# Another list of steps for the main phase of a one-core attention and feed-forward kernel

## The chip, the cores and the metric

The program runs on one core of a Trainium2 chip. The metric is the device time of one execution in microseconds (us), as the median of several executions. Engines are named as in the profile: PE (matmuls), PEld (its weight loads), DVE, ACT, POOL and SP (which issues nearly all DMAs).

## The reference, cut to what matters

A row vector x of width 512 goes through an attention with 32 heads of width 16 that all share one key and one value head, and through a gated feed-forward layer of inner width 1376. A sigmoid gate g, one number for each of the 2048 rows, mixes both.

```python
g = sigmoid((x * gate_w).sum(-1, keepdims=True))
q = (x @ wq).reshape(B, S, H, Dh).transpose(0, 2, 1, 3)      # S 2048, H 32, Dh 16
k, v = x @ wk, x @ wv                                        # one head for all
p = softmax(einsum("bhqd,bkd->bhqk", q, k) * Dh ** -0.5)
a = einsum("bhqk,bkd->bhqd", p, v).transpose(0, 2, 1, 3).reshape(B, S, H * Dh) @ wo
b = (gelu(x @ w_gate) * (x @ w_up)) @ w_down                 # inner width 1376
out = g * a + (1 - g) * b
```

## The kernel before, in words

The rows are cut into four groups of 512. A prologue of some 82 us computes the queries of all groups (written to HBM as `scr`), the keys `kp`, the values `v1` and `v2` and a first piece of the feed-forward layer. Then comes the main phase, which both halves of the reference share, and a short tail (the output projection of the last group).

Attention in the main phase goes by units: a unit `u` is one row group and four of the 32 heads, so there are 32 units, and each runs over 16 key chunks of 128. For a unit and a key chunk there are two **score steps** (letter S in the list). A score step is a pair of matmuls (L751), each on one half of PE's 128 rows, that write 128 x 1024 scores into two banks of PSUM, and one exponential on ACT (L754) that reads them and writes a tile `p`. There are three such bank pairs: numbers 0 and 1 take the scores in turn; number 2 takes them where the list has a Z in place of an S. There are 1024 score steps. Then comes one **value step** (letter V) for each unit and key chunk: four matmuls (L821) beside each other, each on 32 of PE's columns, that add the product of `p` and the values to the unit's accumulator `acc`. There are 512 of them; the profile shows each as 8 matmuls, the program's order as 4. After the last value step of a unit, `norm` copies the accumulator with DVE (L765, L775) and divides by the row sums in further pieces of DVE work, kept in the queue `bg`.

The feed-forward layer and the output projection make 77 **jobs**. A job multiplies two pairs of operands at once, into the banks `z` (bank pair 2) and `y`; numbers are split into a high and a low part, so that each product takes three passes. A **pass step** (letter F, L519) is a pair of matmuls, one for `z` and one for `y`, each on one half of PE's rows. A job goes over its passes twice: in the second half `z` and `y` change places between the two halves of the rows, for which the first matmul of the second half waits for a small memset on POOL (L527) that waits for the first half. There are three kinds of job: gate jobs (24 pass steps, followed by a gelu on DVE and ACT, L544 to L560), down jobs (18 or 12 pass steps, followed by two additions on DVE, L624) and output jobs (24, L634). Weights and rows are split into high and low parts while a job runs: DVE casts the high part (L201), POOL subtracts it (L202); `slot` puts one such piece of work behind every third pass step. At the end of a row group `reload_x` loads the next group's rows as tiles `xst` and splits them into `xh` and `xl` in the same way, during the last two down jobs of the group.

What stands in which order on PE is written out in the table `PLAN`, 78 lines, one for each job and one ahead. `play` reads a line word by word:

```python
            if t[0] in "SZ":
                for _ in range(k):
                    score(t[0] == "Z")
            elif t[0] == "V":
                visit(k)
            elif t[0] == "H":
                ...
                pairs = pair_mm(z, y, X, Y)
            elif t[0] == "F":
                for _ in range(k):
                    next(pairs)
            else:
                job[1](z, y)
```

H opens a job, R closes it (the else branch: DVE's work on `z` and `y` is issued), T issues the gelu's tanh on ACT, and a number behind a letter repeats it. All engines take their instructions in the order in which `play` issues them, so the table sets the order on DVE, ACT, POOL and SP too.

Of the kernel before, what the change touches and what calls it, by code (L numbers as in the profile page):

```python
# [20 lines left out]
S = 2048  # L21
D = 512
H = 32
DH = 16
F = 1376
# [17 lines left out]
PB = 12  # L43
PLAN = [
# [78 lines left out]
]  # L123


# [811 lines left out]
```

## Time and profile before

| | |
|---|---|
| median of 3 runs | 1246.28 us (1244.94 to 1249.26) |
| the profiled execution | 1246.9 us, its span 1244.8 us |
| PE busy | 1237.2 us (99%) |
| ACT busy | 1031.7 us (83%) |
| DVE busy | 526.2 us (42%) |
| POOL busy | 215.6 us (17%) |
| granted PE clock | 0.999 |

The first line holds times of whole executions. The others come from one execution that the profiler recorded. A PE that is busy all the time need not do its work at full pace: a matmul's end is modelled, so the pace is read from the starts of the steps.

### The profile page before, as it was taken

Reading aid. Unit: us, or ns where it says so; the run is one execution under the profiler, and the core shown is the slowest. Engines: PE = TensorE matmul, PEld = TensorE weight load, DVE = VectorE, ACT = ScalarE, POOL = GpSimd, SP = SyncE. Lnnn points to the kernel's source line nnn. Section 1 sums busy time; section 2 is a strip of 40 time slices with the busy share of each in tenths; the row PEclk is TensorE's granted clock in tenths of the full one; section 3 lists DMA queues with packets and bytes.
Section 4 is the critical chain, followed back from the end, with each engine's and each line's share of the span. In section 5 each row is a group of like instructions: output and inputs, shape, how many; then the busy total and the mean of one; then the engine's idle time right before and its main releaser. Section 6 shows DMA issues by size and latency. Waiting matters only on the chain.

```text
span 1244.8 us, 23618 instructions
## 1 busy us (share of the span) xinstructions
PE 1237.2 (99%) x9742; PEld 657.5 (53%) x9742; DVE 526.2 (42%) x844; ACT 1031.7 (83%) x1127; POOL 215.6 (17%) x265
## 2 busy tenths in 40 slices
PE   9999999999999999999999999999999999999998
PEld 6775555454544554545454555554544555455544
DVE  7872553525423144443443234162455126253334
ACT  5448888988888888888888788888889888898894
POOL 5420311212210120211230021120231011121100
PEclk9999999999999999999999999999999999999999
DMA  8541201103201211101210221010211201010000
GB/s 329 193 149 43 83 14 65 40 23 107 73 15 31 70 40 40 65 24 40 89 53 14 74 65 40 14 65 16 92 58 40 74 14 65 14 58 34 14 1 34
DMA packets 28317, 73.89 MB, mean 59 GB/s; under 512 B 4208, under 2 KB 4464, under 8 KB 28208
## 3 DMA queue, kind: packets, MB, share of 16 engines
q1 hardware_dynamic: 27664, 71.32, 17.1%
q8 instruction: 77, 1.26, 0.4%
q0 software_dynamic: 256, 0.79, 0.2%
q10 hardware_dynamic: 288, 0.26, 0.1%
q14 instruction: 32, 0.26, 0.1%
HBM read 57.41 MB, written 14.94 MB: 58 GB/s over the span
## 4 chain that ended last, share of the span: by engine, by line
PE 92%; issue 1%; POOL 0%; DVE 0%; ACT 0%; DMA 0%; SPq 0%; POOLq 0%
PE acc L821 38%; PE s L751 23%; PE y L519 17%; PE z L519 13%; PE wos L504 1%; POOL xl L202 0%; DVE acc L634 0%; DMA Q<-scr 0%; PE wof L504 0%; ACT p L754 0%; SPq L364 0%; ACT sq L551 0%; SPq L363 0%; POOLq L202 0%; POOL mark L527 0%
## 5 line engine op out<-in xcount | busy, mean ns | idle before, releaser
L754 ACT ACTIVATE p<-s 128x1024 f32<-128x1024 f32 x1024 | 977.4, 1026 | 150.3 <-PE s L751 139.7
L821 PE MATMUL acc<-p,v 128*32 128x512 f32 x4096 | 496.4, 599 | 0.0
L751 PE MATMUL s<-Q,kp 51*128 51x512 f32 x2048 | 397.2, 421 | 1.0 <-DMA Q<-scr 0.9
L751 PEld LDWEIGHTS s<-Q,kp 51*128 51x128 f32 x2048 | 183.7, 184 | 258.0 <-ACT p L754 167.3
L821 PEld LDWEIGHTS acc<-p,v 128*32 128x32 f32 x4096 | 106.7, 109 | 239.2 <-issue 231.2
L527 POOL MEMSET mark<- 1x1 f32 x77 | 7.6, 99 | 890.0 <-PE y L519 874.0
L519 PE MATMUL z<-xh,gh 64*128 64x512 f32 x312 | 122.9, 394 | 0.0
L519 PE MATMUL y<-xh,gh 64*128 64x512 f32 x312 | 122.8, 394 | 0.0
L519 PE MATMUL z<-xl,gh 64*128 64x512 f32 x312 | 122.2, 392 | 0.3 <-POOL xl L202 0.2
L519 PE MATMUL y<-xl,gh 64*128 64x512 f32 x312 | 122.4, 392 | 0.0
L544 DVE COPY gs<-z 128x512 f32<-128x512 f32 x39 | 27.0, 692 | 225.4 <-PE z L519 214.9
L519 PE MATMUL z<-xh,gl 64*128 64x512 f32 x312 | 121.9, 391 | 0.0
L519 PE MATMUL y<-xh,gl 64*128 64x512 f32 x312 | 121.9, 391 | 0.0
L202 POOL TENSOR_TENSOR gl<-st,gh 128x512 fp32r<-128x512 f32 x80 | 107.4, 1361 | 36.5 <-DVE gh L201 35.7
L624 DVE SCALAR_TENSOR_TENSOR acc<-z,gc,acc 128x512 f32<-128x512 f32 x24 | 18.0, 751 | 130.9 <-PE z L519 128.3
L519 PE MATMUL z<-dh,hh 64*128 64x512 f32 x176 | 69.2, 393 | 0.0
L519 PE MATMUL y<-dh,hh 64*128 64x512 f32 x176 | 69.1, 393 | 0.0
L519 PE MATMUL y<-dl,hh 64*128 64x512 f32 x176 | 68.9, 392 | 0.0
L519 PE MATMUL z<-dl,hh 64*128 64x512 f32 x176 | 68.9, 391 | 0.0
L519 PE MATMUL z<-dh,hl 64*128 64x512 f32 x176 | 68.8, 391 | 0.0
L519 PE MATMUL y<-dh,hl 64*128 64x512 f32 x176 | 68.7, 391 | 0.0
L519 PEld LDWEIGHTS y<-xh,gl 64*128 64x128 f32 x312 | 57.7, 185 | 8.4
(174 smaller groups left out, 1536.9 us busy)
## 6 DMA issues: line engine op xcount, KB each, us to landing
st<-wf SPq DMA_DIRECT2D x40, 768.0 KB
scr<-q SPq DMA_DIRECT2D x16, 512.0 KB
Q<-scr SPq DMA_DIRECT2D x64, 128.0 KB
Q<-scr SPq DMA_DIRECT2D x64, 64.0 KB
out<-acc SPq DMA_DIRECT2D x16, 256.0 KB
xr<-xT SPq DMA_DIRECT2D x6, 512.0 KB
xst<-xT SPq DMA_DIRECT2D x12, 256.0 KB
st<-wf SPq DMA_DIRECT2D x5, 256.0 KB
```

The lines of the kernel that those rows point to most:

```text
L202: eng_l.tensor_sub(lo, src, hi)
L504: nc.tensor.matmul(ps, a, b, start=(first and q == 0), stop=(last and q == len(terms) - 1), skip_group_check=True)
L519: mm = nc.tensor.matmul(ps, a[rs], b[rs], start=(half == 0 and q == 0), stop=(half == 1 and q == len(X) - 1), skip_group_check=True)
L527: relay = nc.gpsimd.memset(mark, 0.0).ins
L544: nc.vector.tensor_copy(gs, g)
L624: nc.vector.scalar_tensor_tensor(o, ps, w, o, op0=ALU.mult, op1=ALU.add)
L751: nc.tensor.matmul(ps[:, j * TG : (j + 1) * TG], kp[rs, kc * P : (kc + 1) * P], Q[u][rs, pr], start=True, stop=True)
L754: nc.scalar.activation(p, ps, AF.Exp, bias=0.0, scale=SCALE)
L821: nc.tensor.matmul(accp[u][32 * j : 32 * j + 32], vt[:, kc], pb[s, j // 2][:, (j % 2) * TG : (j % 2 + 1) * TG], start=(kc == 0), stop=(kc ...
```

## The change

All 78 lines of `PLAN` are replaced, nothing else. The new lines hold the same numbers of score steps (1024), value steps (512), pass steps (1608) and jobs (77) in the same order of jobs; the steps are interleaved in another way. Two lines out of the 78, the one of the last down job of the second row group and the last one:

```diff
-    "f: H F4 S F2 S V S F6 R S2 V3 S",
+    "f: H F3 S F3 S V S F3 S F3 R S V Z S2 V3 Z S2 V2 S",
...
-    "f: H F3 S F3 S V S F2 S F4 R S V Z S2 V2 S V3",
+    "f: H F5 S F S V S F3 S F3 R S V5",
```

Counted over both tables (S and Z both as score steps; a block is a row of equal steps that follow each other on PE):

| | before | now |
|---|---|---|
| value blocks of 1, 2, 3, 4, 5 steps | 106, 117, 36, 16, 0 | 103, 91, 58, 12, 1 |
| value blocks in all | 275 | 265 |
| score blocks of 1, 2, 3 steps | 634, 54, 94 | 658, 15, 112 |
| pass blocks of 3 steps, of all | 268 of 508 | 362 of 521 |
| places where a score and a pass step meet | 1015 | 1041 |
| score steps in bank pair 2 (Z) | 119 | 112 |

PE at the end of the main phase, from the last pass step on, before. `s` are the banks of the scores, `acc` is the accumulator of the last unit, `wos` the first of the tail's four results:

```order
L519 MATMUL z<-dh_12869,hl_13223 128x512
L519 MATMUL y<-dh_12869,hl_13223 128x512
L751 MATMUL s<-Q_12767,kp 128x512 x2
L821 MATMUL acc_13186<-p,v_76 32x512 x4
L751 MATMUL s<-Q_12767,kp 128x512 x6
L821 MATMUL acc_13186<-p,v_76 32x512 x8
L751 MATMUL s<-Q_12767,kp 128x512 x2
L821 MATMUL acc_13186<-p,v_76 32x512 x12
L504 MATMUL wos_13452<-woh,oh_11623 128x512
```

The same place now:

```order
L519 MATMUL z<-dh_12965,hl_13247 128x512
L519 MATMUL y<-dh_12965,hl_13247 128x512
L751 MATMUL s<-Q_12720,kp 128x512 x2
L821 MATMUL acc_13162<-p,v_76 32x512 x20
L504 MATMUL wos_13452<-woh,oh_11542 128x512
```

Three value blocks of one, two and three steps have become one of five; the sixth value step and four score steps stand further ahead.

DVE at the reload of the third row group's rows, before. `xst2_0` to `xst2_3` are the four loaded pieces of the rows, `xh2` their high parts, `acc14` is the accumulator of unit 14, and the lines L624 are the additions behind the last two down jobs of the second group:

```order
L201 CAST xh2_6864<-xst2_1_6736 128x512
L624 SCALAR_TENSOR_TENSOR acc1_4152<-z_6915,gc_79,acc1_4152 128x512
L624 SCALAR_TENSOR_TENSOR acc1_4152<-y_6916,gc_79,acc1_4152 128x512
L795 CAST oh13_6991<-nt12_6229 128x512
L799 TENSOR_TENSOR ol13_6992<-nt12_6229,oh13_6991 128x512
L765 COPY n014_6995<-acc14_6670 128x512
L201 CAST xh2_6864<-xst2_2_6868 128x512
L201 CAST xh2_6864<-xst2_3_6959 128x512
L766 TENSOR_SCALAR nt14_6996<-n014_6995,mk_80 128x512
```

The same place now:

```order
L795 CAST oh13_7005<-nt12_6220 128x512
L799 TENSOR_TENSOR ol13_7006<-nt12_6220,oh13_7005 128x512
L765 COPY n014_7009<-acc14_6639 128x512
L201 CAST xh2_6911<-xst2_1_6811 128x512
L624 SCALAR_TENSOR_TENSOR acc1_4265<-z_6974,gc_79,acc1_4265 128x512
L624 SCALAR_TENSOR_TENSOR acc1_4265<-y_6975,gc_79,acc1_4265 128x512
L201 CAST xh2_6911<-xst2_2_6915 128x512
L201 CAST xh2_6911<-xst2_3_7026 128x512
L766 TENSOR_SCALAR nt14_7010<-n014_7009,mk_80 128x512
```

The copy of the unit's accumulator stood between the additions of the last down job and the casts of the last two pieces; now it stands ahead of those additions.

144 rows, old and new, of the table PLAN are left out of this document.

## The prediction

> **What bounds the kernel now.** I read the page first, then PE's waits, then the timeline of PE and ACT in a piece of the main phase, last the one place where PE's waits name another engine. The page gives the span, each engine's time and the chain that ended last:
>
> ```profile
> span 1244.8 us, 23618 instructions
> ...
> PE 1237.2 (99%) x9742; PEld 657.5 (53%) x9742; DVE 526.2 (42%) x844; ACT 1031.7 (83%) x1127; POOL 215.6 (17%) x265
> ...
> PE 92%; issue 1%; POOL 0%; DVE 0%; ACT 0%; DMA 0%; SPq 0%; POOLq 0%
> ...
> L754 ACT ACTIVATE p<-s 128x1024 f32<-128x1024 f32 x1024 | 977.4, 1026 | 150.3 <-PE s L751 139.7
> L821 PE MATMUL acc<-p,v 128*32 128x512 f32 x4096 | 496.4, 599 | 0.0
> ```
>
> PE is never idle and makes 92% of the chain. ACT is second: its 1024 exponentials fill 977.4 us, and it stood idle 150.3 us ahead of them, nearly all of it (139.7) until PE had written scores. So ACT waits for PE. PE's own list of waits is short. Its two rows with lines of the main phase (engine and line, what it waited for, total, count, longest):
>
> ```profile
> PE s L751 <- DMA Q<-scr: 0.9, 1, 0.9
> ...
> PE z L519 <- POOL xl L202: 0.2, 1, 0.2
> ```
>
> The first happened once, ahead of the first score steps, and both tables begin alike; no DMA was waited for after that, so SP's changed order costs nothing as long as loads are issued as far ahead as now. The second comes back below. So the main phase is as long as PE's steps at PE's pace, and what a new order of the same steps can change is what PE pays for going from one kind of step to another, and the waits. The timeline of PE shows both prices (start, duration, what, count):
>
> ```profile
> 407.81 0.40 PE L751 MATMUL s<-Q,kp 51*128 51x512 f32 x2
> 408.05 0.39 PE L519 MATMUL z<-woh,oh 64*128 64x512 f32 x1
> ...
> 408.74 0.40 PE L751 MATMUL s<-Q,kp 51*128 51x512 f32 x2
> ...
> 410.61 0.40 PE L751 MATMUL s<-Q,kp 51*128 51x512 f32 x2
> 410.94 2.78 PE L821 MATMUL acc<-p,v 128*32 128x512 f32 x24
> 413.65 0.51 PE L751 MATMUL s<-Q,kp 51*128 51x512 f32 x2
> 413.99 0.39 PE L519 MATMUL y<-woh,oh 64*128 64x512 f32 x1
> ...
> 417.47 0.41 PE L751 MATMUL s<-Q,kp 51*128 51x512 f32 x2
> 417.81 1.07 PE L821 MATMUL acc<-p,v 128*32 128x512 f32 x8
> 418.81 0.97 PE L751 MATMUL s<-Q,kp 51*128 51x512 f32 x6
> 419.71 2.78 PE L821 MATMUL acc<-p,v 128*32 128x512 f32 x24
> 422.42 0.50 PE L751 MATMUL s<-Q,kp 51*128 51x512 f32 x2
> 422.76 0.39 PE L519 MATMUL z<-xh,gh 64*128 64x512 f32 x1
> ```
>
> From the score step at 407.81 to the next at 408.74 lie that step and three pass steps (the first is shown), 0.93 us, 0.2325 each: a score step costs what a pass step costs, and going between the two costs nothing. A value block is different. The chain of waits has blocks of three and of four value steps:
>
> ```profile
> 108.62 2.71 PE acc L821 x24
> 132.75 3.57 PE acc L821 x32
> ```
>
> One more value step is 0.86 us. From 410.61 to 413.99 are two score steps and a block of three: 3.38 - 2 x 0.2325 - 3 x 0.86 = 0.335 us over. From 417.47 to 422.76 are five score steps and blocks of one and three: 5.29 - 5 x 0.2325 - 4 x 0.86 = 0.69, so 0.34 each. If I take the price of a value step from the same rows, (2.71 - 1.00) / 2 = 0.855, the three come to 0.35 each. **A value block costs 0.34 us (0.335 to 0.355) over its steps, however long it is.**
>
> **The change part by part.** Score, value and pass steps are the same in number, so their own time stays.
>
> *Value blocks.* There are 275 in the old table and 265 in the new: 10 x 0.34 = 3.4 us less (3.35 to 3.55). The last line shows how: blocks of one, two and three become one of five. Blocks of four run in the trace of before at 3.57 us without a wait inside; a block of five was not there. Its last step needs the exponential of the last score step, which starts 0.33 + 4 x 0.86 = 3.8 us ahead of it, and an exponential takes 1.026. That is free unless ACT is more than two exponentials behind. The tail behind it is untouched.
>
> *Score and pass steps meet in 1041 places instead of 1015.* By the row of 0.93 us this is free. If each meeting cost half a value block, it would be 26 x 0.17 = 4.4 us, which would eat the whole gain; that is a rival below. The Trainium skill bears on it ("TensorEngine Tiling (Array Packing)", Tiling Modes): a change of the tiling mode drains the array, a change of the tile alone does not. Score and pass steps both use halves of the rows, value steps quarters of the columns; by that rule too only value blocks pay, and the trace agrees (0.93 for four steps against 0.34 over for a block).
>
> *The change of halves inside a job.* Its first matmul waits for POOL's memset. In both tables a value block stands between the halves in 76 jobs, and two score steps alone in one: nothing changes.
>
> *The wait for POOL.* It stands in the first gate job of the third row group:
>
> ```profile
> 625.42 0.40 PE L519 MATMUL z<-xh,gh 64*128 64x512 f32 x1
> ...
> 625.90 0.50 PE L519 MATMUL z<-xl,gh 64*128 64x512 f32 x1
> ...
> 626.25 0.39 PE L519 MATMUL z<-xh,gl 64*128 64x512 f32 x1
> ...
> 626.71 0.39 PE L519 MATMUL z<-xh,gh 64*128 64x512 f32 x1
> ...
> 627.33 0.50 PE L519 MATMUL z<-xl,gh 64*128 64x512 f32 x1 [0.24 <-POOL xl L202]
> ...
> 627.67 0.39 PE L519 MATMUL z<-xh,gl 64*128 64x512 f32 x1
> ```
>
> The first three starts lie 0.48 and 0.35 us apart, the last three 0.62 and 0.34, where 0.2325 is the pace: 0.25 + 0.12 + 0.39 + 0.11 = 0.87 us lost, more than the 0.24 that the view puts down to the wait. The cause is in DVE's and POOL's timelines:
>
> ```profile
> 620.80 0.74 DVE L624 SCALAR_TENSOR_TENSOR acc<-y,gc,acc 128x512 f32<-128x512 f32 x1
> ...
> 623.33 0.69 DVE L765 COPY n<-acc 128x512 f32<-128x512 f32 x1 [0.73 <-PE acc L821]
> 623.94 0.75 DVE L201 CAST xh<-xst 128x512 fp32r<-128x512 f32 x2
> 624.61 1.52 DVE L766 TENSOR_SCALAR nt<-n,mk 128x512 f32<-128x512 f32 x1
> ...
> 624.44 2.84 POOL L202 TENSOR_TENSOR xl<-xst,xh 128x512 fp32r<-128x512 f32 x2 [5.88 <-DVE xh L201]
> ```
>
> The copy of unit 14's accumulator had to wait for PE's value block, and the casts of the last two pieces stood behind it; POOL could begin only at 624.44. In the new order the copy stands ahead of the last job's additions, so the casts no longer wait for it. And the table leaves more time between that job's R and the next job's first passes: before "S2 V3 S", 3 x 0.2325 + 3 x 0.86 + 0.34 = 3.6 us; now "S V Z S2 V3 Z S2 V2 S", 8 x 0.2325 + 6 x 0.86 + 3 x 0.34 = 8.0 us. That is 4.4 us more for pieces that came under 1 us late. I take the whole 0.87 us as gone; were it kept, or were there one at each of the three reloads (the other two show none now), the term would be 0 or a loss of 1.74 us.
>
> A rule of the Trainium skill speaks against counting on this ("SBUF — State Buffer", Who interferes with whom): DVE and POOL share a pair of ports under an exclusive lock, and the later of two instructions that need it is blocked for the whole of the other. The row of L766 shows it: 1.52 us, while POOL ran beside it, against a mean that the groups view gives as
>
> ```profile
> L766 DVE TENSOR_SCALAR nt<-n,mk 128x512 f32<-128x512 f32 x16 | 9.8, 614 | 0.4
> ```
>
> so 0.9 us lost on DVE, and POOL's two pieces kept their pace (2.84 for two). In the new order L766 again stands behind the casts; what it delays is the splitting for the next job, a whole job (24 pass steps, 5.6 us at least) away. By the rule the sum stays, but where another order puts a cast behind a subtraction the 0.87 us may come back somewhere else.
>
> *Sum.* -3.4 - 0.87, with 0.1 kept for small waits that the new order makes: -4.2 us. The profiled execution took 1246.9 us, 0.6 over the median of 1246.28. So 1242.7 for a profiled execution, and **1242.1 us for the median**, 0.34% less. About 0.3% (3.7 us) is what a measurement of this kernel can tell from no change; the forecast lies just beyond that.
>
> **The rivals.** *A, the forecast.* PE's time is the sum of its steps and its value blocks, and the new waits are as rare as the old: 1242.1. Chance 0.77.
>
> *B, the wait for POOL stays or moves.* The blocks' 3.4 us are won, but at one to three of the three reloads a piece comes late again, 0.87 us each: -3.4 + (0 to 1.74), 1242.9 to 1244.6. For it: the port lock, and DVE's order is new around every unit's end. Against it: 4.4 us more time at the one place that waited. Chance 0.14; it is within 0.3%.
>
> *C, slower: score steps wait for their banks.* Blocks of three score steps grow from 94 to 112. The third takes the bank of the score step ahead of the value block, and needs its exponential to have ended. ACT's timeline beside the rows above:
>
> ```profile
> 414.25 4.75 ACT L754 ACTIVATE p<-s 128x1024 f32<-128x1024 f32 x5 [1.84 <-PE s L751]
> 419.41 2.85 ACT L754 ACTIVATE p<-s 128x1024 f32<-128x1024 f32 x3 [0.40 <-PE s L751]
> ```
>
> The third score step of the block at 418.81 starts at 418.81 + 2 x 0.2325 = 419.28; the exponential that frees its bank, the fifth of the row, ended at 419.00. The margin is 0.28 us. If the 18 new blocks met ACT one exponential (4.75 / 5 = 0.95 us) later, each would wait 0.95 - 0.28 = 0.67: 12 us, 1246.3 - 4.2 + 12 = 1254.1. It decides from 0.28 + 4.2 / 18 = 0.5 us of delay on. Against it: the 94 blocks of before all ran without it (PE's waits do not name ACT), ACT's pace of 0.95 for a chained exponential is about that of a score step and three pass steps, 0.93, and 50 of the 77 new job lines end, behind R, word for word like some line of the old. Chance 0.03.
>
> *D, the change doesn't do what the count says.* The 0.34 us are not tied to the block, or each meeting of a score and a pass step costs 0.17 after all: -4.2 + 4.4, 1246.5. The row of 0.93 speaks against it. Chance 0.06, within 0.3%.
>
> **How the numbers follow.** The likeliest is A, 1242.1. The range reaches down to 1240.0: 0.15 for the upper end of a block's price, 0.1 for no new wait, and the 1.3 us that the lowest of the three runs lay under their median, with half a microsecond of small losses of before that I have not named. It reaches up to 1245.8: the upper end of B, 1244.6, and the same scatter. That leaves out C and part of D. A lies only 0.5 us beyond the bound of 0.3%, so I give a seventh of it to "within": faster 0.66, same 0.11 + 0.14 + 0.06 = 0.31, slower 0.03.
>
> **What would show it.** In the profile of the changed kernel: PE's waits name no POOL; a block of three value steps between two score steps again takes 3.38 us from score to pass step; the last block of five takes about 4.4 us; score and pass steps keep 0.23; ACT's idle time ahead of the exponentials falls by some 4 us, since it has the same work in a shorter span. If the block count counts and something else lost, the starts of the steps show gaps over 0.2325 with ACT (C) or POOL (B) named ahead of them. I am wrong if the span is not 3 to 5 us shorter.

## The result, and the profile after

| | before | new list |
|---|---|---|
| median (9 runs each) | 1246.37 us (1244.94 to 1249.26) | 1241.94 us (1241.25 to 1243.3) |
| ratio | 1 | 0.9963, interval 0.9953 to 0.9974 |
| profiled execution, its span | 1246.9 us, 1244.8 us | 1241.9 us, 1239.8 us |

The new list is 0.37% faster; the forecast was 1242.1 us. The page of the new kernel, the lines that answer to those of before:

```profile
span 1239.8 us, 23617 instructions
...
PE 1233.3 (99%) x9742; PEld 658.6 (53%) x9742; DVE 523.8 (42%) x844; ACT 1031.1 (83%) x1127; POOL 214.9 (17%) x265
...
PE 93%; DMA 0%; DVE 0%; ACT 0%; SPq 0%; issue 0%; ACTq 0%
...
L754 ACT ACTIVATE p<-s 128x1024 f32<-128x1024 f32 x1024 | 973.3, 1025 | 130.6 <-PE s L751 126.0
L821 PE MATMUL acc<-p,v 128*32 128x512 f32 x4096 | 494.3, 599 | 0.0
```

PE's waits in the new kernel are these two, and both stand in the prologue or at its seam to the main phase (engine and line, what it waited for, total, count, longest):

```profile
PE s L751 <- DMA Q<-scr: 1.4, 1, 1.4
PE pw L214 <- DVE kmx L215: 1.2, 1, 1.2
```

The row with POOL has gone. To see where the 5.0 us of span come from, the main phase is cut out of PE's timeline, from the first score step to the first matmul of the tail. Before:

```profile
82.24 0.93 PE L751 MATMUL s<-Q,kp 51*128 51x512 f32 x4 [0.95 <-DMA Q<-scr]
...
1226.74 2.78 PE L821 MATMUL acc<-p,v 128*32 128x512 f32 x24
1229.45 0.50 PE L504 MATMUL wos<-woh,oh 128*128 128x512 f32 x1
```

Now:

```profile
81.50 0.93 PE L751 MATMUL s<-Q,kp 51*128 51x512 f32 x4 [1.35 <-DMA Q<-scr]
...
1219.76 0.39 PE L751 MATMUL s<-Q,kp 51*128 51x512 f32 x2
1220.08 4.50 PE L821 MATMUL acc<-p,v 128*32 128x512 f32 x40
1224.51 0.50 PE L504 MATMUL wos<-woh,oh 128*128 128x512 f32 x1
```

From first step to tail: 1229.45 - 82.24 = 1147.21 us before, 1224.51 - 81.50 = 1143.01 now, 4.20 us less. The prologue, which the change does not touch, ended 0.74 us earlier in this one execution, and the rest of the span differs by 0.06. So 4.2 of the 5.0 us belong to the change. (The sections below give the main phase from its first to its last step as 1146.24 and 1142.04; the difference is the same 4.20.) Ten value blocks fewer at 0.34 make 3.4 of it. The rest is gaps. Each start on PE was set against the median for its kind of step and its neighbours; before, 14 starts came more than 0.05 us late, 1.98 us in all, and now 11 do, 1.11 us in all. That is 0.87 less, and the four late starts at the third reload, 0.86 of the 1.98, are gone. With the blocks it makes 4.27 for the 4.20 measured. The last two rows now show the block of five, 1224.51 - 1220.08 = 4.43 us.

At the reload of the third row group, PE's timeline of the new kernel:

```profile
623.82 0.39 PE L751 MATMUL s<-Q,kp 51*128 51x512 f32 x2
624.14 1.06 PE L821 MATMUL acc<-p,v 128*32 128x512 f32 x8
...
629.64 1.92 PE L821 MATMUL acc<-p,v 128*32 128x512 f32 x16
631.50 0.50 PE L751 MATMUL s<-Q,kp 51*128 51x512 f32 x2
631.83 0.40 PE L519 MATMUL z<-xh,gh 64*128 64x512 f32 x1
```

The line's end took 631.83 - 623.82 = 8.0 us, as worked out from the words. DVE and POOL beside it:

```profile
627.96 0.43 DVE L201 CAST xh<-xst 128x512 fp32r<-128x512 f32 x1 [2.19 <-DMA xst<-xT]
...
628.70 1.52 DVE L767 TENSOR_SCALAR nz<-n,mkb 128x512 f32<-128x512 f32 x1
```

```profile
628.46 1.47 POOL L202 TENSOR_TENSOR xl<-xst,xh 128x512 fp32r<-128x512 f32 x1 [1.33 <-DVE xh L201]
```

The last piece now waited for its own load (2.19 us idle on DVE), and POOL finished it at 629.93, 1.9 us before the next job's first step. A DVE instruction beside POOL is again stretched to 1.52 us, L767 this time, and nobody waits for it. With this load the longer line end was needed: 4.4 us earlier, the next job would have started at 627.4, before the load of the last piece had landed. (Whether the load would then have landed earlier too, no run shows.)

### The profile page after: what moved, and what is told of

Same layout as the page of the kernel before. It is cut to its first block, busy times and chain, and to the rows that moved or that the text cites. A ratio compares the mean times of both kernels' runs of the same rounds, so it can differ in the third digit from the quotient of the medians.

```text
span 1239.8 us, 23617 instructions
## 1 busy us (share of the span) xinstructions
PE 1233.3 (99%) x9742; PEld 658.6 (53%) x9742; DVE 523.8 (42%) x844; ACT 1031.1 (83%) x1127; POOL 214.9 (17%) x265
## 4 chain that ended last, share of the span: by engine, by line
PE 93%; DMA 0%; DVE 0%; ACT 0%; SPq 0%; issue 0%; ACTq 0%
PE acc L821 38%; PE s L751 24%; PE y L519 17%; PE z L519 13%; PE wos L504 1%; DMA Q<-scr 0%; DVE acc L634 0%; PE wof L504 0%; ACT p L754 0%; ACT sq L551 0%; SPq L363 0%; ACTq L754 0%
## 5 line engine op out<-in xcount | busy, mean ns | idle before, releaser
L624 DVE SCALAR_TENSOR_TENSOR acc<-z,gc,acc 128x512 f32<-128x512 f32 x24 | 18.0, 751 | 130.6 <-PE z L519 122.6
```

Source lines behind the costliest of these rows:

```text
L624: nc.vector.scalar_tensor_tensor(o, ps, w, o, op0=ALU.mult, op1=ALU.add)
```

## The experiments

The theory: the main phase is PE's steps plus 0.34 us for each value block, plus waits. The rivals are those of the prediction: score steps wait for their banks (C), the 0.34 us are not the block's or the meetings of score and pass steps cost (D), the wait for POOL only moves (B). Each time and ratio is against the kernel before on the same chip. "Main phase" is first score step to last step, from the starts in the profiled execution; in experiments 1 to 4, 8 and 9, which edit the new list, it is compared with the new list's 1142.04 us, in 5 to 7 with the 1146.24 us of before.

**1. More blocks, nothing else.** The new list with 35 of its line ends cut into single value steps: 300 blocks, the same steps.

```diff
-    "... R S V S Z S V3 Z S2 V2 S",
+    "... R S V S Z S V3 Z S V S V S",
```

> The new table with 35 line ends 'S2 V2 S' written as 'S V S V S': the same steps, 300 value blocks instead of 265. Theory (a value block costs 0.34 us, whatever its length): 35 x 0.34 = 11.9 us more than the new table's 1241.9, so 1253.8, a ratio of 1.006 to the kernel before. Rival (the gain came from something else that goes with the new table, such as the wait for POOL or the spacing of the scores): no change, 1242, ratio 0.9965.

1254.88 us (1252.95 to 1256.71), ratio 1.0069, interval 1.0054 to 1.0085. The main phase is 1153.41 us, 11.4 more than with the new list, 0.325 for each added block. (By the ratios it is some 13 us; the four executions here lie 3.8 us apart, and the profiled one is the fastest.) PE's waits name nothing in the main phase. One such line end in PE's timeline:

```profile
618.84 0.39 PE L751 MATMUL s<-Q,kp 51*128 51x512 f32 x2
619.16 1.06 PE L821 MATMUL acc<-p,v 128*32 128x512 f32 x8
620.15 0.73 PE L751 MATMUL s<-Q,kp 51*128 51x512 f32 x4
620.82 1.07 PE L821 MATMUL acc<-p,v 128*32 128x512 f32 x8
621.81 0.50 PE L751 MATMUL s<-Q,kp 51*128 51x512 f32 x2
622.24 1.07 PE L821 MATMUL acc<-p,v 128*32 128x512 f32 x8
623.24 0.50 PE L751 MATMUL s<-Q,kp 51*128 51x512 f32 x2
```

The price can be read in its parts. A score step ahead of a block takes 0.32 to 0.33 (618.84 to 619.16), 0.10 over its 0.2325. A block of one value step takes 1.00, 0.14 over 0.86. The score step behind a block and ahead of the next takes 0.43 (621.81 to 622.24), 0.10 over for each side. 0.10 + 0.14 + 0.10 = 0.34.

**2. The same place, the blocks as they were, but a score step more between a block and the next job.** 265 blocks; the second score step of the end has to wait until the exponential has cleared its bank.

```diff
-    "... R S V S Z S V3 Z S2 V2 S",
+    "... R S V S Z S V3 Z S V2 S2",
```

> The new table with the same 35 line ends 'S2 V2 S' written as 'S V2 S2': 265 value blocks as in the new table, one score step moved behind the block. Theory with blocks alone: no change, 1241.9, ratio 0.9965. Rival C (score steps wait for their banks) at this place: behind the block come two score steps and three pass steps, then a score step that takes the bank of the first of the two. It is due 0.34 + 0.23 + 0.70 = 1.27 us after the first; that one's exponential starts some 0.6 after it and takes 1.03, so the bank is free at about 1.63 to 1.70, a wait of 0.36 to 0.43. Where the next line closes that gap, 35 x 0.4 = 14 us: 1256, ratio 1.008, with PE's waits or gaps behind ACT.

1263.19 us (1262.09 to 1263.34), ratio 1.0128, interval 1.0113 to 1.0144. So rival C's mechanism is real where an order provokes it. PE's waits:

```profile
PE s L751 <- ACT p L754: 8.9, 35, 0.5
```

That is 35 places, as many as were edited, but 8.9 us, where the main phase is 20.3 us longer. One place in PE's timeline, and ACT's beside it:

```profile
464.34 0.39 PE L519 MATMUL z<-xh,gl 64*128 64x512 f32 x1
...
464.99 0.50 PE L751 MATMUL s<-Q,kp 51*128 51x512 f32 x2 [0.26 <-ACT p L754]
465.32 0.40 PE L519 MATMUL z<-xh,gh 64*128 64x512 f32 x1
```

```profile
463.91 3.78 ACT L754 ACTIVATE p<-s 128x1024 f32<-128x1024 f32 x4 [0.57 <-PE s L751]
```

From the start of the last pass step to that of the score step are 0.65 us where 0.2325 is the pace: 0.42 lost, though the row names 0.26. And the score step behind the stop takes 0.33 instead of 0.23. So about 0.42 x 35 = 14.7, 0.105 x 35 = 3.7 for the step behind each stop, and 1.7 at the ends of 12 value blocks, 20.1 of the 20.3 measured. My expectation was right in direction and too low, because it left out the step behind the stop and those ends.

**3. Fewer meetings of score and pass steps.** 13 lines changed, 1015 meetings, as before the change, instead of 1041; 265 blocks.

```diff
-    "f: H F3 S F3 S V S F3 S F3 R S V S Z S V2 S",
+    "f: H F6 S2 V S F3 S F3 R S V S Z S V2 S",
```

> The new table with 13 pieces 'F3 S F3 S V S' written as 'F6 S2 V S': 265 value blocks, but score and pass steps meet in 1015 places as in the old table, not in 1041. Theory (meeting places are free): 1241.9, ratio 0.9965. Rival D (each costs half a value block, 0.17 us): 26 x 0.17 = 4.4 us less, 1237.5, ratio 0.993.

1241.79 us (1240.98 to 1243.3), ratio 0.9962, interval 0.9949 to 0.9976; the main phase 1142.08 against 1142.04. The 26 meetings cost nothing, and D, which wanted 4.4 us, is refuted.

**4. Fewer blocks at the price of a wait.** 14 line ends joined into one longer block, 251 blocks; a Z now stands close behind the R whose bank it takes.

```diff
-    "... R S V Z S2 V3 Z S2 V3 S",
+    "... R S Z S2 V4 Z S2 V3 S",
```

> The new table with 14 pieces 'R S V Z S2 Vn' written as 'R S Z S2 Vn+1': 251 value blocks. If only their number counted: 14 x 0.34 = 4.8 us less, 1237.2, ratio 0.9926. Theory with the wait that such a merge uncovers: the Z score step takes the bank pair that DVE still copies for the closed job. The copy starts 0.43 us after the last pass step and takes 0.69, so the bank is free 1.17 after it; Z would be due 0.23 + 0.23 = 0.47 after it and waits 0.7. 14 x (0.7 - 0.34) = 5 us more, 1247, ratio 1.0005, and a little more if the fourth score step in a row waits for its own bank.

1252.54 us (1251.76 to 1253.46), ratio 1.0044, interval 1.0028 to 1.0059: slower than before with 24 blocks fewer. PE's waits name what took the place of the blocks:

```profile
PE s L751 <- DVE acc L624: 5.5, 9, 0.6
PE s L751 <- DVE acc L622: 1.9, 3, 0.6
...
PE s L751 <- DVE acc L634: 1.2, 2, 0.6
```

One of the 14, on PE and on DVE:

```profile
620.64 0.39 PE L519 MATMUL z<-dh,hl 64*128 64x512 f32 x1
620.87 0.39 PE L751 MATMUL s<-Q,kp 51*128 51x512 f32 x2
621.88 1.09 PE L751 MATMUL s<-Q,kp 51*128 51x512 f32 x6 [0.62 <-DVE acc L624]
```

```profile
621.07 0.75 DVE L624 SCALAR_TENSOR_TENSOR acc<-z,gc,acc 128x512 f32<-128x512 f32 x1 [2.72 <-PE z L519]
```

DVE reads `z` until 621.82, so the Z step started 1.01 us after the S instead of 0.23: 0.775 lost, 14 x 0.775 = 10.85. The steps behind the stop lose some 0.1 each, about 3 us in all, and 14 x 0.34 = 4.8 is won: 9.1 against 9.35 measured. My expectation, 5 us, again left out the steps behind the stop, and it put the wait itself at 0.7.

**5. The wait for POOL alone.** The old list, but the casts of the last two pieces are issued between the two additions of the closing down job, ahead of the accumulator's copy.

```diff
-                w = gc[:, 4 * tg + k : 4 * tg + k + 1]
+                w = (k == 3 and len(batch) == 2 and flush(todo)) or gc[:, 4 * tg + k : 4 * tg + k + 1]
```

> The old table, with the last two casts of a reload issued between the two additions of the last down job, so that DVE's queue has them ahead of the copy of the unit's accumulator. Theory: the gaps of 0.87 us in the first gate job of the third row group go and PE's waits name no POOL; value blocks stay at 275. 0.87 us is 0.07%, too little for a time, so the starts on PE decide. Rival (the port lock or the loads, not DVE's order, made the pieces late): the gaps stay.

One execution: 1245.01 us, against 1245.81 (1245.39 to 1247.45) for the kernel before beside it. One time is too little for a difference of 0.8, so the trace decides. PE's waits name no POOL. The main phase is 1145.49, 0.75 less than before. The last three passes in the first half of that job, where before the wait stood, on PE, and what went ahead of them on DVE and POOL:

```profile
625.20 0.40 PE L519 MATMUL z<-xh,gh 64*128 64x512 f32 x1
...
625.44 0.40 PE L519 MATMUL z<-xl,gh 64*128 64x512 f32 x1
...
625.68 0.39 PE L519 MATMUL z<-xh,gl 64*128 64x512 f32 x1
```

```profile
620.87 0.83 DVE L201 CAST xh<-xst 128x512 fp32r<-128x512 f32 x1 [0.81 <-DMA xst<-xT]
...
624.71 0.49 DVE L766 TENSOR_SCALAR nt<-n,mk 128x512 f32<-128x512 f32 x1
```

```profile
621.78 1.28 POOL L202 TENSOR_TENSOR xl<-xst,xh 128x512 fp32r<-128x512 f32 x1 [0.36 <-DVE xh L201]
```

The passes lie 0.24 apart again; at most 0.16 of the 0.87 us was left in that job. So the term of 0.87 was what its place said, and in the old list DVE's order was its cause.

**6 and 7. Which half of the list does it.** The first 60 lines of the new list with the last 18 of the old (268 blocks), and the reverse (272 blocks). At the seam one score step moves, so that the count of steps fits.

```diff
  6, the first line of the old part:
-    "w: H F3 S F3 S F3 S F3 S V S F S F5 S F5 S F R S V2 S Z S V4 S2",
+    "w: H F3 S F3 S F3 S F3 S V S F S F5 S F5 S F R S V2 S Z S V4 S",
  7, the last line of the old part:
-    "... R S V Z S V2 T S Z S V2 Z S V2 S Z S V2 S",
+    "... R S V Z S V2 T S Z S V2 Z S2 V2 S Z S V2 S",
```

> The first 60 lines of the new table, then the last 18 of the old one with one score step less in the line behind the seam, so that all counts are kept: 268 value blocks. It has 7 of the 10 blocks that went and the place where POOL was waited for. Theory: 7 x 0.34 + 0.87 = 3.3 us less than the kernel before, 1243.1, ratio 0.9974. Rival (the gain comes from the end of the table, with its single block of five): near 1246, ratio 1.

> The first 60 lines of the old table with one score step more in the line ahead of the seam, then the last 18 of the new one: 272 value blocks and the old place where POOL was waited for. Theory: 3 x 0.34 = 1.0 us less than the kernel before, 1245.4, ratio 0.9992. Rival (the gain comes from the end of the table): near 1242, ratio 0.9965.

New first: 1243.01 us (1242.53 to 1244.95), ratio 0.998, interval 0.9971 to 0.9989; main phase 3.23 us less than before, of 3.3 expected. Old first: 1244.97 (1244.57 to 1246.33), ratio 0.9994, interval 0.9985 to 1.0003; main phase 0.79 less, of 1.0. A new gap of 0.29 at the seam is in it: a block of three score steps there takes 1.18 us (957.97 to 959.15), where the one ahead of it takes 0.89. PE's waits of the second name POOL again:

```profile
PE z L519 <- POOL xl L202: 0.2, 1, 0.2
```

Seven blocks and the wait's removal came with the first part, three blocks with the second. Each interval leaves out its rival (a ratio of 1 for the first, 0.9965 for the second), but the two overlap, so it is the main phases that tell the parts apart: 3.23 + 0.79 + 0.29 = 4.31 for the 4.20 us. The gain is spread over the list as the count says.

**8. How much ACT can be late.** A small copy on ACT behind every second exponential, 512 in all, in the new kernel.

```diff
-        pb[s, pr] = p
+        pb[s, pr] = p; n % 2 == 1 and nc.scalar.copy(mark2, bcol)
```

> The new table, with a small extra ACT instruction (a copy of 128 x 1 numbers to a tile that nobody reads) behind every second exponential, 512 in all. It asks how near ACT is to setting the pace. I take 0.2 us for each, an estimate from no row: 102 us more on ACT, which stood idle 130.6 us ahead of its exponentials. If idle time could be used anywhere (ACT is far from the bound): no change, 1242. Theory with the margins of the rows (a chained exponential starts about 0.91 to 0.95 after the one ahead, a score step comes every 0.93 in pass stretches): ACT falls behind by up to 0.1 for each score step there, 8 in a stretch, against a margin of 0.28 at a block of three score steps; waits of PE for ACT appear, some 3 to 12 us, 1245 to 1254.

1242.19 us (1241.52 to 1243.11), ratio 0.9972, interval 0.9961 to 0.9983; main phase 0.46 us longer. The waits that I expected did not come: the load was smaller than I had put it. ACT's timeline:

```profile
404.07 1.94 ACT L754 ACTIVATE p<-s 128x1024 f32<-128x1024 f32 x2
405.89 0.20 ACT L755 COPY mark<-bcol 128x1 f32<-128x1 f32 x1
405.97 1.96 ACT L754 ACTIVATE p<-s 128x1024 f32<-128x1024 f32 x2
```

Each copy shows 0.20 us but takes only 0.08 to 0.09 of ACT's queue: 405.97 - 404.07 = 1.90 for two exponentials and a copy, against 2 x 0.905 for two chained ones. So about 44 us of ACT's work were added, not 100, and they went into its idle time. This run alone could not tell the theories apart.

**9. Twice that.** The copy behind every exponential, 1024 in all.

```diff
-        pb[s, pr] = p
+        pb[s, pr] = p; n >= 0 and nc.scalar.copy(mark2, bcol)
```

> As e6, but with the small ACT instruction behind every exponential, 1024 in all. In e6 two exponentials and one such instruction took 1.90 us from start to start instead of 2 x 0.91 (404.07 to 405.97), so each takes 0.08 to 0.09 us of ACT's queue, not 0.2. Theory: an exponential then comes every 0.99 to 1.0 us, a score step every 0.93 in pass stretches; over the 8 of a stretch ACT falls 0.5 to 0.6 us behind, more than the margin of 0.28 that a block of three score steps had. PE's waits now name ACT; if the 112 blocks of three wait 0.2 to 0.3 us each: 22 to 34 us, 1264 to 1276, ratio 1.014 to 1.024. Rival (ACT's idle time of some 130 us, of which these take 90, absorbs it as it did in e6): 1242, ratio 0.997.

1253.36 us (1252.92 to 1254.54), ratio 1.0051, interval 1.0034 to 1.0068: between the two expectations. Exponentials now follow each other at 0.99 us, and the groups view still shows ACT idle ahead of them:

```profile
L754 ACT ACTIVATE p<-s 128x1024 f32<-128x1024 f32 x1024 | 1034.0, 1040 | 71.5 <-PE s L751 62.0 <-DMA Q<-shs 6.1
```

PE's waits name ACT once, for 0.2 us, but the main phase is 10.4 us longer. The loss lies in some 100 places of about 0.1 us, as here on PE:

```profile
846.02 0.51 PE L751 MATMUL s<-Q,kp 51*128 51x512 f32 x2
...
846.36 0.39 PE L519 MATMUL y<-xl,gh 64*128 64x512 f32 x1
```

0.34 where 0.23 is the pace, with no wait named, as behind the stops of experiment 2. The exponential that clears the bank of this score step, and PE's weight loads at the same place, show what happened:

```profile
844.88 1.08 ACT L754 ACTIVATE p<-s 128x1024 f32<-128x1024 f32 x1
```

```profile
846.02 0.19 PEld L751 LDWEIGHTS s<-Q,kp 51*128 51x128 f32 x2 [0.28 <-ACT p L754]
846.13 0.19 PEld L519 LDWEIGHTS y<-xl,gh 64*128 64x128 f32 x1
...
846.36 0.19 PEld L519 LDWEIGHTS y<-xh,gl 64*128 64x128 f32 x1
```

The exponential ended at 845.96, and the score step and the load of its weights started together at 846.02, where a load otherwise runs 0.23 ahead of its step. The step was within 0.01 us of its time; the next load came 0.11 later, and the next step 0.23 behind that load. With each score step set against the exponential that clears its bank, over the whole trace, 97 of them start within 0.1 us of its end, against 6 with the new list alone, and 10.2 us are lost at the 97, against 0.9 at the 6. So the loss is a wait for ACT, but of the weight load, where PE's waits do not show it. 89 of the 97 stand behind a pass step, and only one is the third step of a block of three, where the expectation had put them. So C's mechanism does decide at some delay, but here every exponential had to be slowed from 0.905 to 0.99 us, and a place then lost a tenth of a microsecond.

## Why the prediction was right

The mechanism held, term by term. That the forecast came within 0.2 us of the median is partly luck, since executions of one kernel lie 2 to 4 us apart; the main phase, 4.20 us less, is the better test.

- **PE's steps and its blocks set the time.** Right. Main phase by number of blocks: 265 in 1142.04, 268 in 1143.00, 272 in 1145.45, 275 in 1146.24, 300 in 1153.41 us. Taking the 0.87 us of POOL's wait from the third and fourth, a line from the first point goes up by 0.32, 0.36, 0.33 and 0.325 for a block.
- **The block's price, 0.34 us.** Right, 0.325 to 0.335 by experiment 1, with its parts seen. The Trainium skill's rule ("TensorEngine Tiling (Array Packing)", Tiling Modes), that a change of mode drains the array and a change of the tile alone does not, agrees at both ends: 0.34 for a block, and nothing for 26 meetings (experiment 3).
- **The wait for POOL, 0.87 us.** Right in size: the late starts fell by 0.87 us, experiment 5 got at least 0.71 of it in that job by DVE's order alone, and where the old lines stand there (experiment 7), it is back. Of the two reasons that the prediction gave, the new order of DVE and the 4.4 us more at the line's end, no run parts what each does in the new list. The margin was smaller than I had it: the last cast stood idle 2.19 us for its load, which I had not priced, and of the more than 3 us that pieces under 1 us late should have had to spare, 1.9 remained.
- **Rival B.** It did not come. The stretch beside POOL that spoke for it is in the trace again (1.52 us for L767), on an instruction that nobody waits for.
- **Rival C.** The mechanism is real (experiments 2 and 9); the new list hardly reaches it: at three of its 112 blocks of three the next start is 0.05 to 0.07 us late. Two readings of the prediction were off, both to C's favour. The step behind a value block takes 0.33, so the third step of its example starts at 419.37 and the margin is 0.37, not 0.28. And its pace of 0.95 holds one exponential's whole duration; exponentials that wait for nothing start 0.905 apart, faster than the 0.93 in which PE gives them work. Where C was forced, a place cost 0.42 us and 0.11 behind it; the price of 0.67, for a delay of a whole exponential, was not tried.
- **Rival D.** Refuted by experiments 1 and 3.
- **The points to look for.** The block of five took 4.43 us of 4.4, the pace and the waits came out as said. The term for ACT was mis-read: I said its idle time ahead of the exponentials would fall by some 4 us, and that row fell by 19.7. ACT's groups show why:

```profile
L551 ACT ACTIVATE sq<-sq 128x512 f32<-128x512 f32 x40 | 25.2, 629 | 19.7 <-DVE sq L548 19.7
```

This row, the gelu's tanh, had 4.9 us before. Both together went from 155.2 to 150.3, 4.9 less. The sum was right; 14.8 us of idle time only moved from the exponentials to the tanh, which now stands in ACT's queue ahead of its data more often, and PE waits for none of it.

## What to carry to other kernels

Where one engine is never idle, list what it pays for going from one kind of work to another, read the price from the starts of the steps (their durations and the waits view both hide it), and count such changes in the old and the new order: here 10 x 0.34 us gave most of 4.2 us. Fewer changes are worth their price only while nothing else is provoked: 24 fewer than before lost 5.4 us, since a step then stood too close behind the DVE work that frees its bank. A wait's cost is more than the view's figure: 0.24 named for 0.87 lost, 8.9 for 20.

## What the runs showed of the hardware

- The start that follows a stop of PE comes about 0.10 us late (0.33 to 0.34 instead of 0.23): behind the 35 stops for ACT in experiment 2, behind those for DVE in experiment 4, and inside the 0.87 us. It is as much as behind a value block, and the weight loads show where it lies. In the new kernel's trace 2346 of the 2367 score and pass steps that follow one another have their weights loaded 0.2 us or more ahead of their start. At all 529 seams between score or pass steps and value blocks the first load starts with its step (0.002 us ahead), as it does behind the stops, and at the 97 places of experiment 9 it runs at most 0.04 ahead. By the trace, what is lost is the load's lead; why the load cannot run ahead at a seam it does not show. So a step can cost its neighbour 0.10 us without PE being seen to wait.
- A small instruction on ACT costs its queue less than it shows: 0.20 us shown, 0.08 to 0.09 taken. Exponentials that follow each other without a wait start 0.905 us apart though each lasts 1.025. A load worked out from shown durations is too high by that much; mine for experiment 8 was.
